# Both heads of a sorted pair in one transfer, and the decode steps of the seventh pair at other places

## The chip, the cores and the metric

The kernel runs on one core of a Trainium2 chip. The metric is the time of the program on the device in microseconds (us), lower is better. Beside it stand profiled executions, whose span runs from the first to the last instruction.

## The reference

Clustered attention, then a feed-forward block with hard-swish. Queries, keys and values are (batch 4, heads 8, 768 rows, 64 wide), with 16 centroids for each head.

```python
def _attn_ref(q, k, v, centroids):
    B, H, S, D = q.shape                       # 4, 8, 768, 64
    scale = 1.0 / np.sqrt(D)
    # q_n, k_n, c_n: rows divided by their norms
    q_assign = np.argmax(np.einsum('bhsd,hcd->bhsc', q_n, c_n), axis=-1)
    k_assign = np.argmax(np.einsum('bhsd,hcd->bhsc', k_n, c_n), axis=-1)
    mask = q_assign[:, :, :, None] == k_assign[:, :, None, :]
    scores = np.where(mask, scale * np.matmul(q, k.transpose(0, 1, 3, 2)), -1e9)
    attn = softmax(scores)                     # over the keys
    return np.matmul(attn, v)

def _moe_ref(x, w_in, w_out):                  # x: (3072, 512), from (B, S, H * D)
    h = x @ w_in                               # 512 -> 2048
    g = h * np.clip(h + 3.0, 0.0, 6.0) / 6.0
    return g @ w_out                           # 2048 -> 512
```

The weights w_in and w_out arrive as 64-bit floats and the kernel turns them into 32-bit floats itself.

## The kernel before

**Pairs.** The 32 heads are worked in 16 pairs. Two heads lie side by side on TensorE's 128 rows, and four pairs make the 512 inputs of one batch of the feed-forward block. Pairs 0 to 7 (the first two batches) take the full masked attention; pairs 8 to 15 are sorted by cluster first and then need only a band of the scores.

**The first stage, pairs 0 to 7.** A loop runs over n in steps of two, twelve values of n for each pair, so a pair has six double steps r = 0, 2, ... 10. A double step issues two blocks of scores (`ps`, L400, which takes one of two PSUM buffers), their exponentials on ScalarE (`ex`, L423), sums of the exponentials over the keys on GpSimd (`acc`, L430 and L433), and, two blocks later, the product with the values (`pv`, L443). Between them stand:
- the preparation of the next pair: transposes at r = 0 and 2 (`pqk`, L320), cluster scores at r = 4 (`pcs`, L337), the choice of the cluster at r = 6 (`route`: `pr` on TensorE, L348, then `mx` and `one_hot` on VectorE, L351 and L357), and the transposes of the one-hots at r = 8 and 10 (`po`, L379);
- the division, at r = 2 and 8: sums over partitions (`pd`, L467), a reciprocal and a product on VectorE (`rcp` L473, `num` L474). One double step later the result goes to memory, and ScalarE checks the reciprocals' range in place (L488, L489);
- the decode of the weights: 32 chunks of five steps each, `split` (L232 on VectorE, L228 on ScalarE, and the load of the chunk after next), `join` (L238), `power` (L248, and L244 on ScalarE), `rest` (L254), `total` (L259), and four weight sums after them. The table in `share` says how many steps a double step takes. They are issued at the end of the double step, behind its preparation;
- some up-projections of the first feed-forward block (`ph`, L607), at fixed n.

**The second stage, pairs 8 to 15.** Feed-forward items stand in a list, `fill`: for each block of tokens eight up-projections (`uX` and `uY`, L659) in a form that needs sums of weights (`tx`, loaded from `td` by ScalarE's queue, L548, two items ahead), and seven parts of the down-projection (`X` and `Y`, L698). One item is issued at each point of a plan, `late_plan`, and around it the steps of the sorted pairs, which `steps_of` places by hand: each pair starts 28 points after the last one. For a pair they are, in order: load the natural rows of q and k (`piece`), transpose them (`ps`, L919), cluster scores and choice, ranks (`order`, `positions`); load q, k and v again by rows (`qn`, `kvn`); scatter them to memory in sorted order (GpSimd, `scatter`, L1034); load the sorted rows (`piece`, `vs`), transpose, band attention, store the sorted result, gather it back (GpSimd, L1050), transpose and store for the feed-forward block.

**The order is written out by hand.** All is inside `tc.manual_schedule()`: each engine runs its instructions in the order of the program, and a transfer that waits in SP's queue holds up all behind it. Transfers from SP and from ScalarE take eight completion semaphores in turn, in the program's order.

**Loads of natural rows.** Each was one transfer for each head t of the pair, 192 KB. For the keys and values there were two steps, one for each head:

```python
for a, x in enumerate((k, v)):
    nc.sync.dma_start(st["kvn", g][:, :, t, a], natural(x, g, t))
```

Of the kernel before, what the change touches and what calls it, by code (L numbers as in the profile page):

```python
# [18 lines left out]
P = 128  # L19
# [100 lines left out]
def fast_path(ctx, tc, ok, q, k, v, centroids, moe_w_in, moe_w_out, out):  # L120
# [3 lines left out]
    nc = tc.nc  # L124
# [53 lines left out]
    st = {}  # L178
# [698 lines left out]
        for g in range(FIRST, NPAIR) for t in range(2) for name, w in (("qd", D), ("kvd", 2 * D), ("xsd", D))  # L877
    }

    def natural(x, g, t):  # L880
        b, h = divmod(2 * g, H)
        return x[b, h + t].rearrange("(p j) d -> p j d", p=P)

    def ranked(name, g, t, part=0):
        return rows[name, g, t].rearrange("(i p) d -> p i d", p=P)[:, :, part * D : (part + 1) * D]

    def load_piece(key, src):
        piece = st[key] = st["piecep"].tile([P, NCH, 2, D], F32, name="piece")
        for t in range(2):
            nc.sync.dma_start(piece[:, :, t], src(t))  # L890

    def load_natural(g, a):
        x = (q, k)[a]
        load_piece(("qk"[a] + "nat", g), lambda t: natural(x, g, t))

    def load_queries(g):
        qn = st["qn", g] = st["fromp"].tile([P, 2, NCH, D], F32, name="qn")
        for t in range(2):
            nc.sync.dma_start(qn[:, t], natural(q, g, t))

    def load_keys(g, t):
        if t == 0:
            st["kvn", g] = st["fromp"].tile([P, NCH, 2, 2, D], F32, name="kvn")
        for a, x in enumerate((k, v)):
            nc.sync.dma_start(st["kvn", g][:, :, t, a], natural(x, g, t))

    def load_ranked(g, a):
        if a < 2:
            load_piece(("qk"[a] + "s", g), lambda t: ranked(("qd", "kvd")[a], g, t))
            return  # L910
        vs = st["vs", g] = st["svp"].tile([P, 2, NCH, D], F32, name="vs")
        for t in range(2):
            nc.sync.dma_start(vs[:, t], ranked("kvd", g, t, 1))
# [278 lines left out]
    def steps_of(g):  # L1192

        first, last = g == FIRST, g == NPAIR - 1
        f = -3 if first else -5
        if first:
            plan = [
                (-38, load_queries), (-37, load_keys, 0), (-36, load_keys, 1), (-37, run_up),
                (-36, step_up), (-31, order), (-30, positions), (-20, lambda g: st.pop("signed")()),
            ]  # L1200
        else:
            plan = [
                (-46, load_natural, 0), (-45, load_natural, 1), (-38, turn_natural, 0), (-37, turn_natural, 1),
                (-36, cluster_scores), (-34, own_clusters), (-33, run_up), (-32, step_up), (-32, load_queries),
                (-31, load_keys, 0), (-29, order), (-29, positions), (-29, load_keys, 1),
            ]
        plan += [
            (-29 if first else -24, scatter, 0), (-29 if first else -24, scatter, 1), (-12, band_masks), (f, load_ranked, 0), (f, load_ranked, 1),
            (f + 1, load_ranked, 2), (-1, turn_ranked, 0), (0, turn_ranked, 1),
        ]  # L1210
        d = 1 if last else 2
        plan += [
            (d, band_scores, (0, 5), 1), (d + 2, band_scores, (2,), 3), (d + 4, band_scores, (4,)),
            (d + 4, band_values, 0), (d + 4, key_adds, 0, 1, 2), (d + 5, key_adds, 0, 3), (d + 7, band_values, 1),
            (d + 7, key_adds, 1, 1, 2), (d + 8, key_adds, 1, 3), (d + 10, band_sums),
            (12 if last else 14, band_divide), (14 if last else 16, keep_ranked),
            (15 if last else 23, gather), (28 if last else 37, turn_back),
        ]
        return [(g, *step) for step in plan]
# [28 lines left out]
    per_pair = 2 * NCH  # L1248
# [12 lines left out]
    READY, DECODED = per_batch + 2 * lag_d, 2 * per_batch  # L1261

    def share(n, r):


        if n < READY:
            return {0: 4, 2: 3, 4: 3, 6: 1, 8: 2, 10: 4}[r]
        if n < DECODED - per_pair:
            return {0: 6, 2: 5, 4: 4, 6: 3, 8: 5, 10: 5}[r]
        return {0: 6, 2: 5, 4: 4, 6: 1, 8: 3, 10: 4}[r]  # L1270

    HOLD = 6
# [13 lines left out]
    with tc.manual_schedule():  # L1286
# [19 lines left out]
        for n in range(0, total + lag_d + 2, 2):  # L1306
            g, r = divmod(n, per_pair)
# [25 lines left out]
            if n < total:  # L1333
                for step in decode[: share(n, r)]:
                    step()
                del decode[: share(n, r)]
# [389 lines left out]
```

## Time and profile before

| | us |
|---|---|
| median of three runs | 949.89 |
| lowest and highest | 947.76, 950.37 |
| profiled execution, its own time | 947.94 |
| its span, first to last instruction | 946.1 |
| TensorE busy | 928.3 |
| VectorE busy | 591.6 |
| GpSimd busy | 583.9 |
| ScalarE busy | 349.5 |

The granted TensorE clock was 0.998. In the profile PE is TensorE, PEld its weight loads, DVE VectorE, ACT ScalarE, POOL GpSimd, and SP the engine that only issues transfers; SPq and ACTq are the queues in which SP and ScalarE issue transfers and wait for semaphores. L12 is line 12 of the kernel before. A row of a timeline has start, duration, engine, line, operation, what it writes and reads, shapes and a count; in brackets at the end stands the idle time before it and what ended that. In a row of waits stand the total, how often, and the longest.

### The profile page before, as it was taken

What the parts mean: (1) busy time and instruction counts of PE and PEld (TensorE: products, weight loads), DVE (VectorE), ACT (ScalarE), POOL (GpSimd) and SP (SyncE); (2) the same over time, 40 slices, a digit from 0 to 9 for tenths busy, and PEclk for the clock granted to TensorE, in tenths of its full rate; (3) what the DMA queues carried; (4) which work ended last, traced back from release to release, by engine and by line L of the source; (5) the groups of instructions that cost most, each with busy time, mean ns of one, the idle gap of its engine ahead of it and who ended that gap; (6) DMA issues with size and microseconds to landing.
All of it is one profiled execution on the core that took longest, in us unless ns stands there. A gap on an engine that the chain in (4) does not pass through costs nothing.

```text
span 946.1 us, 17635 instructions
## 1 busy us (share of the span) xinstructions
PE 928.3 (98%) x6358; PEld 726.5 (77%) x6358; DVE 591.6 (63%) x1294; ACT 349.5 (37%) x731; POOL 583.9 (62%) x1314
## 2 busy tenths in 40 slices
PE   8999999989999999999999999999999999999997
PEld 5444444555798798797887988978888799999996
DVE  6789889899976375284483474564571554536261
ACT  5888877766112232233232132241331311212020
POOL 3878777769366677787777777777777060303030
PEclk9999999999999999999999999999999999999999
DMA  7345555361364648482683654754753233323120
GB/s 192 108 134 157 134 156 165 109 174 46 96 209 141 153 137 175 130 220 78 171 201 100 166 158 128 192 151 113 176 161 99 77 99 113 106 69 110 56 68 26
DMA packets 174351, 124.23 MB, mean 131 GB/s; under 512 B 134064, under 2 KB 152496, under 8 KB 174256
## 3 DMA queue, kind: packets, MB, share of 16 engines
q1 hardware_dynamic: 151936, 76.04, 31.2%
q10 hardware_dynamic: 13104, 34.38, 12.7%
q0 software_dynamic: 9216, 12.60, 4.4%
q8 instruction: 52, 0.85, 0.4%
q14 instruction: 43, 0.35, 0.1%
HBM read 94.67 MB, written 28.31 MB: 130 GB/s over the span
## 4 chain that ended last, share of the span: by engine, by line
PE 70%; DVE 2%; DMA 1%; ACT 0%; POOL 0%; issue 0%; SPq 0%; ACTq 0%
PE Y L698 18%; PE uY L659 15%; PE X L698 13%; PE uX L659 12%; PE pv L1116 3%; PE ps L1077 3%; PE ps L919 2%; PE pv L1077 1%; PE pd L1140 1%; PE pcs L337 1%; PE ps L1157 1%; DMA piece<-kvd 1%; DVE g_sb L649 0%; DVE g_sb L502 0%; DVE g_sb L670 0%; DVE sx L670 0%
## 5 line engine op out<-in xcount | busy, mean ns | idle before, releaser
L433 POOL TENSOR_TENSOR acc<-acc,ex 128x768 f32<-128x768 f32 x64 | 123.8, 1935 | 26.0 <-ACT ex L423 22.4
L1034 POOL DMA_INDIRECT qd<-qn,pos x96 | 96.3, 1003 | 44.9 <-issue 32.5
L1050 POOL DMA_INDIRECT xn<-xsd,pos x96 | 93.7, 976 | 48.8 <-DVE g_sb L649 27.1
L499 ACT ACTIVATE sx<-g_sb,half_c 128x512 f32<-128x512 f32 x88 | 63.7, 724 | 141.1 <-DVE g_sb L670 141.1
L649 POOL TENSOR_TENSOR g_sb<-g_sb 128x256 f32<-128x256 f32 x52 | 39.1, 773 | 123.6 <-DVE g_sb L502 122.6
L1034 POOL DMA_INDIRECT kvd<-kvn,pos x96 | 96.6, 1006 | 25.6 <-issue 25.6
L1026 POOL MEMSET w_low<- 128x1 f32 x864 | 90.9, 105 | 33.3
L705 DVE TENSOR_TENSOR y<-y,Y 128x256 f32<-128x256 f32 x48 | 20.2, 421 | 136.5 <-PE Y L698 135.7
L659 PE MATMUL uX<-xb,w_in_sb 128*128 128x128 f32 x704 | 93.0, 275 | 0.0
L698 PE MATMUL X<-w_out_sb,g_sb 128*128 128x256 f32 x384 | 90.6, 382 | 0.4 <-DVE g_sb L502 0.4
L698 PE MATMUL Y<-T,g_sb 128*128 128x256 f32 x384 | 88.0, 381 | 0.0
L698 PE MATMUL Y<-w_out_sb,g_sb 128*128 128x256 f32 x384 | 87.7, 380 | 0.0
L659 PEld LDWEIGHTS uX<-xb,w_in_sb 128*128 128x128 f32 x704 | 85.7, 192 | 0.0
L698 PEld LDWEIGHTS X<-w_out_sb,g_sb 128*128 128x128 f32 x384 | 70.9, 190 | 14.8 <-issue 3.9
L698 PEld LDWEIGHTS Y<-T,g_sb 128*128 128x128 f32 x384 | 72.1, 190 | 13.2 <-issue 3.9
L670 DVE TENSOR_TENSOR sx<-uX,sx 128x128 f32<-128x128 f32 x176 | 51.0, 290 | 49.3 <-ACT sx L677 45.7
L698 PEld LDWEIGHTS Y<-w_out_sb,g_sb 128*128 128x128 f32 x384 | 71.9, 190 | 10.6 <-issue 1.3
L400 PE MATMUL ps<-xf 64*128 64x384 f32 x384 | 78.6, 487 | 0.3 <-ACT ex L423 0.3
L423 ACT ACTIVATE ex<-ps 128x768 f32<-128x768 f32 x96 | 72.6, 802 | 4.6 <-PE ps L400 4.5
L443 PE MATMUL pv<-ex,vt 128*64 128x384 f32 x384 | 72.5, 499 | 0.0
L502 DVE SCALAR_TENSOR_TENSOR g_sb<-sx,g_sb 128x512 f32<-128x512 f32 x88 | 63.6, 725 | 3.4 <-ACT sx L499 3.4
L670 DVE TENSOR_TENSOR g_sb<-uY,sx 128x128 f32<-128x128 f32 (+1 forms) x176 | 65.5, 413 | 0.0
(196 smaller groups left out, 1805.5 us busy)
## 6 DMA issues: line engine op xcount, KB each, us to landing
tx<-td ACTq DMA_DIRECT2D x86, 384.0 KB, 3.5
raw<-in_moe_w_in_dram SPq DMA_DIRECT2D x16, 512.0 KB, 3.8
raw<-in_moe_w_out_dram SPq DMA_DIRECT2D x16, 512.0 KB, 3.2
xb<-xd SPq DMA_DIRECT2D x12, 512.0 KB, 4.3
out_dram<-y SPq DMA_DIRECT2D x44, 128.0 KB, 1.7
qk<-in_q_dram SPq DMA_DIRECT2D x18, 192.0 KB, 3.7
qk<-in_k_dram SPq DMA_DIRECT2D x18, 192.0 KB, 5.0
vt<-in_v_dram SPq DMA_DIRECT2D x16, 192.0 KB, 3.8
```

The lines of the kernel that those rows point to most:

```text
L400: nc.tensor.matmul(st["ps", n][:, t, 0:HALF], lhsT=x[r, NCH + j], rhs=x[r, hf * NHC : (hf + 1) * NHC], start=first, stop=last, skip_group_ ...
L423: nc.scalar.activation(out=ex, in_=sc, func=ACT.Exp, scale=SM_SCALE)
L433: nc.gpsimd.tensor_tensor(out=acc, in0=acc, in1=ex, op=ALU.add)
L443: nc.tensor.matmul(pv[t * D : (t + 1) * D], lhsT=vt[:, t, j], rhs=ex[:, t], start=(j == 0), stop=(j == NCH - 1),)
L499: nc.scalar.activation(out=r, in_=h, func=ACT.Relu, bias=half_c, scale=1.0 / 6.0)
L502: nc.vector.scalar_tensor_tensor(out=g, in0=r, scalar=1.0, in1=h, op0=ALU.min, op1=ALU.mult)
L659: nc.tensor.matmul(dst, lhsT=w[:, kt], rhs=x(kt), start=(kt == 0), stop=(kt == HK - 1))
L670: nc.vector.tensor_tensor(out=out_, in0=in0, in1=in1, op=ALU.add)
L698: nc.tensor.matmul(bank[:, half * HC : (half + 1) * HC], lhsT=g_sb[:, kind, i], rhs=w[:, i], start=(first and i == 0), stop=(last and i == ...
L1026: nc.gpsimd.memset(w_low, W_LOW)
L1034: i = nc.gpsimd.indirect_dma_start(out=rows[name, g, t], in_=src, in_offset=None, out_offset=bass.IndirectOffsetOnAxis(ap=pos[:, a, j, t : ...
L1050: nc.gpsimd.indirect_dma_start(out=xn[:, j, t], out_offset=None, in_=rows["xsd", g, t], in_offset=bass.IndirectOffsetOnAxis(ap=pos[:, 0, j ...
```

## The change

First, `natural` gives both heads of a pair at once, and the natural rows, queries, keys and values of a sorted pair are each loaded by one transfer of 384 KB instead of two of 192 KB. The two steps of `load_keys`, which loaded keys and values of head 0 and then of head 1, now load the keys of both heads and then the values of both; they stay at their points of the plan. The sorted rows (`ranked`) are still loaded head by head.

Second, the seventh pair (n from 72 to 83) gets a row of its own in the table of decode steps. The fifth pair's end and the sixth keep the old row.

```diff
-    def natural(x, g, t):
+    def natural(x, g, order="p j t d"):
         b, h = divmod(2 * g, H)
-        return x[b, h + t].rearrange("(p j) d -> p j d", p=P)
+        return x[b, h : h + 2].rearrange(f"t (p j) d -> {order}", p=P)
...
-    def load_piece(key, src):
+    def new_piece(key):
         piece = st[key] = st["piecep"].tile([P, NCH, 2, D], F32, name="piece")
-        for t in range(2):
-            nc.sync.dma_start(piece[:, :, t], src(t))
+        return piece
 
     def load_natural(g, a):
-        x = (q, k)[a]
-        load_piece(("qk"[a] + "nat", g), lambda t: natural(x, g, t))
+        nc.sync.dma_start(new_piece(("qk"[a] + "nat", g)), natural((q, k)[a], g))
 
     def load_queries(g):
         qn = st["qn", g] = st["fromp"].tile([P, 2, NCH, D], F32, name="qn")
-        for t in range(2):
-            nc.sync.dma_start(qn[:, t], natural(q, g, t))
-
-    def load_keys(g, t):
-        if t == 0:
+        nc.sync.dma_start(qn, natural(q, g, "p t j d"))
+
+    def load_keys(g, a):
+        if a == 0:
             st["kvn", g] = st["fromp"].tile([P, NCH, 2, 2, D], F32, name="kvn")
-        for a, x in enumerate((k, v)):
-            nc.sync.dma_start(st["kvn", g][:, :, t, a], natural(x, g, t))
+        nc.sync.dma_start(st["kvn", g][:, :, :, a], natural((k, v)[a], g))
...
+        if n < DECODED - 2 * per_pair:
+            return {0: 6, 2: 5, 4: 4, 6: 3, 8: 5, 10: 5}[r]
         if n < DECODED - per_pair:
-            return {0: 6, 2: 5, 4: 4, 6: 3, 8: 5, 10: 5}[r]
+            return {0: 8, 2: 3, 4: 3, 6: 2, 8: 4, 10: 8}[r]
         return {0: 6, 2: 5, 4: 4, 6: 1, 8: 3, 10: 4}[r]
```

More of the change, by code (lines that the diff above doesn't have):

```diff
@@ L878, in fast_path @@
     }
-    def natural(x, g, t):
+    def natural(x, g, order="p j t d"):
         b, h = divmod(2 * g, H)
-        return x[b, h + t].rearrange("(p j) d -> p j d", p=P)
+        return x[b, h : h + 2].rearrange(f"t (p j) d -> {order}", p=P)
     def ranked(name, g, t, part=0):
         return rows[name, g, t].rearrange("(i p) d -> p i d", p=P)[:, :, part * D : (part + 1) * D]
-    def load_piece(key, src):
+    def new_piece(key):
         piece = st[key] = st["piecep"].tile([P, NCH, 2, D], F32, name="piece")
-        for t in range(2):
-            nc.sync.dma_start(piece[:, :, t], src(t))
+        return piece
     def load_natural(g, a):
-        x = (q, k)[a]
-        load_piece(("qk"[a] + "nat", g), lambda t: natural(x, g, t))
+        nc.sync.dma_start(new_piece(("qk"[a] + "nat", g)), natural((q, k)[a], g))
     def load_queries(g):
         qn = st["qn", g] = st["fromp"].tile([P, 2, NCH, D], F32, name="qn")
-        for t in range(2):
-            nc.sync.dma_start(qn[:, t], natural(q, g, t))
-    def load_keys(g, t):
-        if t == 0:
+        nc.sync.dma_start(qn, natural(q, g, "p t j d"))
+    def load_keys(g, a):
+        if a == 0:
             st["kvn", g] = st["fromp"].tile([P, NCH, 2, 2, D], F32, name="kvn")
-        for a, x in enumerate((k, v)):
-            nc.sync.dma_start(st["kvn", g][:, :, t, a], natural(x, g, t))
+        nc.sync.dma_start(st["kvn", g][:, :, :, a], natural((k, v)[a], g))
     def load_ranked(g, a):
         if a < 2:
-            load_piece(("qk"[a] + "s", g), lambda t: ranked(("qd", "kvd")[a], g, t))
+            piece = new_piece(("qk"[a] + "s", g))
+            for t in range(2):
+                nc.sync.dma_start(piece[:, :, t], ranked(("qd", "kvd")[a], g, t))
             return
```

## The prediction

> **What bounds the kernel now.** I read the page first, then what TensorE waited for, then the timeline of each engine around the two longest of those waits, then the chain of waits.
>
> ```profile
> span 946.1 us, 17635 instructions
> ...
> PE 928.3 (98%) x6358; PEld 726.5 (77%) x6358; DVE 591.6 (63%) x1294; ACT 349.5 (37%) x731; POOL 583.9 (62%) x1314
> ...
> PE Y L698 18%; PE uY L659 15%; PE X L698 13%; PE uX L659 12%; PE pv L1116 3%; PE ps L1077 3%; PE ps L919 2%; PE pv L1077 1%; PE pd L1140 1%; PE pcs L337 1%; PE ps L1157 1%; DMA piece<-kvd 1%; DVE g_sb L649 0%; DVE g_sb L502 0%; DVE g_sb L670 0%; DVE sx L670 0%
> ```
>
> TensorE is busy for 928.3 of 946.1 us, and the diff takes no matmul away. So the change can move only the 17.8 us in which TensorE is idle. The profiled run took 947.94 us, 1.84 more than its span; the median of the three runs is 949.89, 1.95 above that run. I work out a difference and put it on the median.
>
> What TensorE waited for (total, times, longest) has two waits of 2 us, and both stand at things that the diff touches:
>
> ```profile
> PE po L379 <- DVE one_hot L357: 2.5, 2, 2.3
> PE uX L659 <- DMA tx<-td: 2.0, 1, 2.0
> ```
>
> The 2.3 us wait lies in the seventh pair: the turn of the routed one-hots (po) waits for VectorE. The 2.0 us wait lies among the sorted pairs: the weight sums tx come late, for a reason shown below.
>
> **Part one: the decode steps of the seventh pair.** Its six double steps (r = 0, 2, ... 10) held 6, 5, 4, 3, 5, 5 steps and now hold 8, 3, 3, 2, 4, 8: 28 both times, so nothing is added. Two steps go from r = 2 to r = 0, one from r = 4 to r = 6, two from r = 6 to r = 8, three from r = 8 to r = 10. The steps that load raw weights (every fifth) keep their places, so SP's queue is the same here. VectorE, whose queue the steps are moved in, now:
>
> ```profile
> 182.79 0.69 DVE L248 TENSOR_SCALAR wunit<-wtop 128x512 uint32<-128x512 uint32 x1
> 183.40 2.55 DVE L473 RECIPROCAL rcp<-pd 128x384 f32<-128x384 f32 x1
> 185.98 0.67 DVE L474 TENSOR_TENSOR num<-num,rcp 128x384 f32<-128x384 f32 x1
> 186.57 2.31 DVE L254 SCALAR_TENSOR_TENSOR wunit<-raw,wunit 128x512 f32<-128x512 uint32 x1
> ...
> 194.98 0.55 DVE L351 TENSOR_REDUCE mx<-pr 128x24 f32<-128x384 f32 x1
> 195.57 0.62 DVE L357 TENSOR_TENSOR one_hot<-pr,mx 128x192 bf16<-128x192 f32 x2
> ```
>
> The routing (mx, one_hot) starts only when VectorE has worked off the steps ahead of it, at 194.98. TensorE, ScalarE and GpSimd meanwhile:
>
> ```profile
> 189.64 0.55 PE L348 MATMUL pr<-ident,cs 128*128 128x128 f32 x3
> 190.12 0.34 PE L400 MATMUL ps<-xm 64*128 64x384 bf16 x2
> ...
> 193.18 0.81 PE L467 MATMUL pd<-acc,ones 128*64 128x384 f32 x4
> 196.25 0.51 PE L379 MATMUL po<-ident_q,one_hot 128*128 128x128 bf16 x6 [2.26 <-DVE one_hot L357]
> ```
>
> ```profile
> 187.66 0.51 ACT L488 ACTIVATE rcp<-rcp 128x384 f32<-128x384 f32 x1
> ...
> 188.90 1.49 ACT L423 ACTIVATE ex<-ps 128x768 f32<-128x768 f32 x2
> ```
>
> ```profile
> 182.51 8.05 POOL L433 TENSOR_TENSOR acc<-acc,ex 128x768 f32<-128x768 f32 x4
> 190.53 1.82 POOL L430 TENSOR_TENSOR acc<-ex 128x768 f32<-128x768 f32 x1
> ```
>
> L254, which reads two SBUF tiles, takes 2.31 while one of GpSimd's sums runs; L248, which reads one, takes 0.69, and I take that for an L254 that meets no sum. The four sums of the row take 2.01 each, so they end near 184.4, 186.5, 188.4 and 190.5.
>
> The new order, by these rows (a step of 0.69 is followed by the next after 0.6 to 0.7): L248 at 182.79; L254 at 183.5, held by the first sum to 184.4, ends 184.9; L259; the reciprocal at 185.5 instead of 183.40, because two decode steps now stand ahead of it; it ends at 188.1. L474 also reads two SBUF tiles and is held until the third sum ends: 188.85 instead of 186.65. Behind it wait two others. pr needs the PSUM buffer that the reciprocal frees: 188.1 is before 189.64, 1.5 us of room, free. ScalarE's in-place L488 waits for L474, and behind it in ScalarE's queue stand the exponentials: 187.66 becomes 188.95, so ex goes from 188.90 to 190.2 and its first half ends near 190.95. TensorE's ps, at 190.12 now, needs that half's buffer: it stalls 0.83 us, a wait that is new. VectorE goes on with L232, L238, L248 (188.9 to 191.05); its L254 then meets no sum, since L430 needs the delayed exponentials and starts after 191.6; L259 and L232 follow, and mx at 193.1, one_hot done at 194.3. TensorE finishes pd at 193.99 + 0.83 = 194.82 and finds one_hot ready. The stall goes from 2.26 to 0.83: **1.4 us gained**. From both sides: with L254 and L474 free of every sum, ex would be about 0.8 earlier and 2.2 us gained; with the second L254 held as long as in the row (2.31), one_hot would be done at 195.9 and 0.3 gained.
>
> [...]
>
> Later steps of the pair: the reciprocal of r = 8 comes two steps earlier, the three steps pushed to r = 10 stand behind a clip instead of ahead of it. VectorE has 196.1 to 212 to absorb them; nothing, unless it runs over, then 0.7 per step.
>
> **Part two: one transfer for both heads.** In the built program the transfers of SP and ScalarE take eight semaphores in turn, in program order: each waits until the eighth before it has landed. Five transfers go from each of seven pairs and three from the first sorted pair, 38 in all (403 to 365); bytes and piece sizes stay. The chain of waits, and SP's and ScalarE's queues, before the second wait:
>
> ```profile
> 476.28 4.90 DMA piece<-kvd
> 481.18 0.03 ACTq L548
> ```
>
> ```profile
> 475.70 1.43 SPq L890 DMA_DIRECT2D piece<-kvd  x2
> 477.19 2.15 SPq L913 DMA_DIRECT2D vs<-kvd  x2
> 479.50 1.26 SPq L899 DMA_DIRECT2D qn<-in_q_dram  x2
> 480.93 0.55 SPq L905 DMA_DIRECT2D kvn<-in_k_dram  x1
> 481.53 0.64 SPq L905 DMA_DIRECT2D kvn<-in_v_dram  x1
> ```
>
> ```profile
> 478.53 0.72 ACT L499 ACTIVATE sx<-g_sb,half_c 128x512 f32<-128x512 f32 x1 [2.57 <-DVE g_sb L670]
> 481.24 0.33 ACTq L548 DMA_DIRECT2D tx<-td  x1
> ```
>
> ```profile
> 486.04 0.68 PE L659 MATMUL uX<-xs,tx 128*128 128x128 f32 x4 [2.00 <-DMA tx<-td]
> ...
> 487.45 0.82 PE L919 MATMUL ps<-ident,piece 128*128 128x128 f32 x6
> ```
>
> ScalarE comes to this tx at 478.53 and issues it at 481.24, when a piece<-kvd lands that tx neither reads nor writes. That piece is the eighth before it: kvd, vs, the tx before this one, vs, qn, qn, k, v. Now qn is one transfer, k one for both heads, and the values come after the tx; the eighth before it is a tx, the last but one, that was issued ahead of the whole burst. So tx is issued 2.65 us earlier, at 478.6. It took at most 4.80 beside this burst (481.24 to 486.04); it lands by 483.4, and TensorE would want it at 484.04. **2.0 us gained**; if the burst held it to 6.1 us, 1.4.
>
> What is moved: the values of head 0 come one step later, with those of head 1, and the scatter of the tenth pair, whose queue (POOL's) goes on without rest, could wait for them:
>
> ```profile
> 311.14 0.65 SPq L905 DMA_DIRECT2D kvn<-in_v_dram  x1
> ```
>
> ```profile
> 314.79 0.95 POOL L1034 DMA_INDIRECT kvd<-kvn,pos  x1 [0.63 <-issue]
> ```
>
> The last value transfer was issued at 311.14, so the scatter has 3.6 us already; a landing like that tx's, 4.8, would cost GpSimd 1.2. Pieces like those issued from 475.70 on are turned at 487.45 (L919), 12 us behind their issue, so this hardly reaches the end. But TensorE, which gains, comes up to 3 us earlier against loads that GpSimd paces, and the later tx of the same bursts then wait a little for their eighth; I set **0.4 us** against the gain for that, between 0 and 1.3 (4.80 less the median 3.5 of a tx, in a row below).
>
> Sum: -1.4 - 2.0 + 0.4 = **-3.0 us**: 944.9 for the profiled run, **946.9** on the median, 0.32% less. About 0.3% (2.85 us) is what a measurement can tell from no change, so the forecast sits almost on that edge.
>
> **The rivals.** *tx was late by the crowd, not by the turn.* All 16 engines work through the burst; issued earlier, tx would just take longer. Then part one alone: -1.4, 948.5. For it: the 4.80 beside the burst. Against it: 2.65 us of waiting that the chain puts on another transfer.
>
> *The seventh pair only changes its wait.* If L488 comes later still, ps stalls for all that po gains: -2.0 + 0.4, 948.3. For it: 0.83 of new stall in my own working. Against it: it would take another 1.4 us on that path.
>
> *More goes than the profile shows.* The median run is 1.95 longer than the profiled one. If that, or most of it, is more waits of tx for their turn, which come and go between runs, 38 fewer transfers take 1.5 of it too: 945.4. For it: a wait of 2.65 that hangs on microseconds. Against it: nothing in one profile tells what other runs lose.
>
> *Slower: larger transfers crowd out tx.* In all a tx takes less than that one did:
>
> ```profile
> tx<-td ACTq DMA_DIRECT2D x86, 384.0 KB, 3.5
> ```
>
> So a burst costs it 1.3. If k and v of double size cost it 1.3 again each, that is 2.6 a burst, less the cover: from 478.53, when it can be issued, to 484.04, when it is wanted, are 5.5 us, 0.7 more than 4.80. About half of the eight pairs' bursts should meet up-projections (uX, uY: 27% of the chain, against 31% of the down product X, Y). So 4 x 1.9 = 7.6, less the 1.4 of part one: +6.2, 956.1. It decides from where each of four tx comes 1.8 later: 4 x 1.1 - 1.4 = +3.0.
>
> [...] No run here shows a transfer of both heads.
>
> **The chances.** Forecast 0.52, of it 0.38 beyond 0.3% and 0.14 within, as it sits on the edge; more goes 0.13, beyond; tx late by the crowd 0.12 and the seventh pair's new wait 0.08, both within; crowded out 0.15, of it 0.12 slower and 0.03 within. So faster 0.51, same 0.37, slower 0.12. The range: its low end has the more-goes case with the upper bound of part one (2.2 for 1.4) and nothing given back (945.4 - 0.8 - 0.4), and 0.4 for the spread of runs: 943.8; its high end lies 1.3 above no change, where the crowding has eaten both gains and one tx's delay more: 951.2.
>
> **What would show it.** Right: no wait of uX for tx near 484, tx issued when ScalarE is ready; po's wait gone, a wait of 0.8 of ps for ex at 190.9; 38 fewer issues, the same packets; TensorE busy 928. Wrong: po still waiting a microsecond or more, uX waits of 1 us in other bursts, or TensorE's idle time above 17.8.

## The result, and the profile after

The changed kernel takes **946.54 us** (median of six runs, 945.05 to 949.63); the kernel before, run beside it, 950.29 (six runs, 947.76 to 951.08). The ratio is 0.9963 with a 95% interval of 0.9948 to 0.9977, 3.5 us less. That is the predicted size, but the first profile does not show it where the prediction put it: the profiled execution was the longest of the six (949.63), while that of the kernel before lay at the short end of its own (947.94). The page of the changed kernel, and its waits of TensorE:

```profile
span 947.8 us, 17575 instructions
...
PE 929.6 (98%) x6358; PEld 728.1 (77%) x6358; DVE 589.8 (62%) x1294; ACT 349.5 (37%) x731; POOL 581.5 (61%) x1314
```

```profile
PE uX L659 <- DMA tx<-td: 2.2, 1, 2.2
PE ps L400 <- ACT ex L423: 2.1, 4, 0.8
PE uX L659 <- DVE sx L670: 1.9, 1, 1.9
```

The wait of `po` (2.3) is gone and a wait of `ps` for `ex` has come (0.8 the longest): part one, as forecast. But two waits of `uX` stand where there was one. TensorE's timeline at the three places, 190.97, 484.42 and 547.70 us:

```profile
190.97 0.34 PE L400 MATMUL ps<-xm 64*128 64x384 bf16 x2 [0.83 <-ACT ex L423]
...
194.03 0.81 PE L467 MATMUL pd<-acc,ones 128*64 128x384 f32 x4
194.78 0.51 PE L379 MATMUL po<-ident_q,one_hot 128*128 128x128 bf16 x6
...
484.42 0.68 PE L659 MATMUL uX<-xs,tx 128*128 128x128 f32 x4 [1.90 <-DVE sx L670]
484.94 1.67 PE L659 MATMUL uX<-xb,w_in_sb 128*128 128x128 f32 x8
...
547.70 0.68 PE L659 MATMUL uX<-xs,tx 128*128 128x128 f32 x4 [2.16 <-DMA tx<-td]
```

The wait at 484.42 is put down to VectorE, yet it is `tx` again: this `tx` landed at 484.28, 0.14 before the matmul, the same 0.14 that lies between the landing at 547.56 and 547.70. In the repetition on the first chip the same `uX` starts at 481.78, and the same instruction of VectorE only at 483.29, so the matmul does not need it. The releaser that the profile names can be a bystander that ended at the same moment.

ScalarE's timeline shows that `tx` no longer waits for its turn: it is issued 0.10 after ScalarE comes to it, where the kernel before waited 2.7 us. The windows show what followed the stall:

```profile
477.02 0.72 ACT L499 ACTIVATE sx<-g_sb,half_c 128x512 f32<-128x512 f32 x1 [2.57 <-DVE g_sb L670]
477.12 0.34 ACTq L548 DMA_DIRECT2D tx<-td  x1
```

```profile
484.00:485.20 1.20, 0.78 (x7) 0.81 (x8) 1.17 (x6) 0.00 (x0) 1.06 (x2) 1.00 1.07 276
485.20:488.60 3.40, 3.40 (x24) 3.28 (x23) 1.56 (x4) 1.67 (x3) 2.92 (x8) 0.50 0.65 188
488.60:495.00 6.40, 6.40 (x61) 6.13 (x60) 5.45 (x17) 1.73 (x4) 4.31 (x16) 1.00 0.32 86
```

(columns: window, its length, busy time of TensorE, weight load, VectorE, ScalarE, GpSimd, then TensorE's granted clock, the DMA share and GB/s; the DMA share adds up the packets' own times and can pass 1). So `tx` took 7.16 us to its landing, 477.12 to 484.28, and 7.30 to the matmul, where the kernel before had 4.66 and 4.80, and behind the stall the clock was halved for 3.4 us. Set side by side instruction by instruction, TensorE loses 1.28 us there against the kernel before. The two profiles differ by 1.69 us: -1.47 at `po`, -0.10 at the first `uX`, +1.28 by the clock, +2.16 at 547.70 and -0.37 from a wait of `ps` for `xsort` that is gone (0.4 in the waits of before) make +1.50. One execution of each is not the medians, and the experiments had to show what the typical run gains.

### The profile page after: what moved, and what is told of

It reads as the page before. It is cut to its first block, busy times and chain, and to the rows that moved or that the text cites. A ratio compares the mean times of both kernels' runs of the same rounds, so it can differ in the third digit from the quotient of the medians.

```text
span 947.8 us, 17575 instructions
## 1 busy us (share of the span) xinstructions
PE 929.6 (98%) x6358; PEld 728.1 (77%) x6358; DVE 589.8 (62%) x1294; ACT 349.5 (37%) x731; POOL 581.5 (61%) x1314
## 3 DMA queue, kind: packets, MB, share of 16 engines
q1 hardware_dynamic: 151328, 76.04, 31.2%
## 4 chain that ended last, share of the span: by engine, by line
PE 71%; DVE 2%; DMA 1%; POOL 0%; issue 0%; ACT 0%; ACTq 0%
PE Y L698 18%; PE uY L659 16%; PE X L698 13%; PE uX L659 12%; PE pv L1114 3%; PE ps L917 3%; PE ps L1075 3%; PE pv L1075 1%; DMA tx<-td 1%; PE pd L1138 1%; PE pcs L337 1%; PE ps L1155 1%; PE rk L999 0%; DVE g_sb L649 0%; DVE g_sb L670 0%; PE pdt L1151 0%
```

## The experiments

They ran on three chips in sets of four, each set with the kernel before beside it: 950.79 us on the first (25 runs), 954.79 on the second (35 runs, 948.8 to 960.4), 949.78 on the third (31 runs). Only kernels of one set are compared by their medians.

### First chip: each part alone, and both kernels again

The new share table in the kernel before:

```diff
+        if n < DECODED - 2 * per_pair:
+            return {0: 6, 2: 5, 4: 4, 6: 3, 8: 5, 10: 5}[r]
         if n < DECODED - per_pair:
-            return {0: 6, 2: 5, 4: 4, 6: 3, 8: 5, 10: 5}[r]
+            return {0: 8, 2: 3, 4: 3, 6: 2, 8: 4, 10: 8}[r]
```

> Part one alone: the kernel before with the new decode steps of the seventh pair, every transfer as it was. Prediction's theory: the wait of po for one_hot falls from 2.26 us to about 0, ps waits 0.83 us for ex, 1.4 us gained in this place, so 948.8 beside 950.3. The rival that the sorted pairs' stalls depend on small shifts of time: the place gains its 1.4 us all the same, but the whole may fall anywhere within 2 us of that.

The loads of the changed kernel with the old table:

```diff
-            return {0: 8, 2: 3, 4: 3, 6: 2, 8: 4, 10: 8}[r]
+            return {0: 6, 2: 5, 4: 4, 6: 3, 8: 5, 10: 5}[r]
```

> Part two alone: both heads in one transfer, decode steps as before. By the turn of the eight semaphores (prediction): tx is issued when ScalarE is ready and uX does not wait for it, 1.6 to 2.0 us gained, 948.5. By the crowd on the DMA engines: tx is issued earlier and lands no earlier, uX waits 2 us as before, no change, 950.3. In both the wait of po for one_hot stays at 2.26.

The changed kernel as it is:

> The changed kernel again, for a second profile of it. If the two waits of uX (1.90 and 2.16 us) and the 3.4 us at half clock of its first profile belong to every execution, they show again and the time is that of the first profile, 949.6. If they come and go, this profile has less than 2 us of such waits and the time is near the median, 946.5.

And the kernel before as it is:

> The kernel before again, unchanged, for a second profile of it and for the spread of the measurement. If the stalls of the sorted pairs come and go between executions, a profile of a typical execution (950.3 against 947.94 of the first profile) shows about 2.4 us more of waits for tx than the first one's 2.0. If not, the idle time of TensorE is again 17.8 us. Ratio 1.000 within 0.2%.

| kernel | median us | ratio to before, 95% interval |
|---|---|---|
| share table alone | 948.69 | 0.9982, 0.9973 to 0.9991 |
| loads alone | 948.48 | 0.9973, 0.9962 to 0.9983 |
| both (the changed kernel) | 945.91 | 0.9955, 0.9942 to 0.9968 |
| the kernel before again | 951.37 | 1.0006, 0.9994 to 1.0019 |

Both parts gain, and within these intervals they add up: 1.7 and 2.6 us by the ratios, 4.3 together and 4.3 measured. The waits of TensorE with the share table alone have part one as forecast, and the old wait for `tx`:

```profile
PE ps L400 <- ACT ex L423: 2.1, 4, 0.8
...
PE uX L659 <- DMA tx<-td: 2.0, 1, 2.0
```

The kernel before and the changed one, each profiled again, show that the waits for `tx` are not fixed: 3.1 here for before (2.0 in its first profile, so 1.1 more of the 2.4 more that were expected), and for the changed kernel 1.2 in all, with none near 484:

```profile
PE uX L659 <- DMA tx<-td: 3.1, 1, 3.1
PE po L379 <- DVE one_hot L357: 2.5, 2, 2.3
```

```profile
span 943.1 us, 17575 instructions
...
PE ps L400 <- ACT ex L423: 2.2, 4, 0.8
...
PE uX L659 <- DMA tx<-td: 1.2, 1, 1.2
```

With the loads alone the profile (950.31, its longest run) has the 2.26 of `po` with half a clock behind it, and waits of `uX` of 0.83, 1.47 and 1.23:

```profile
PE uX L659 <- DVE steps L950: 2.7, 2, 1.5
...
PE uX L659 <- DMA tx<-td: 0.8, 1, 0.8
```

The two that are put down to VectorE are waits for `tx` again, which landed 0.14 us ahead of either matmul (487.24 for 487.38, 548.00 for 548.14). So the first profile was no exception: a `tx` that is issued in time can still come late in the merged bursts. The expectation for this kernel had only two cases, no wait of `uX` or the old 2 us; the profile shows neither.

### Second chip: tx earlier, and the turn put back

`tx` three items ahead of its use instead of two, in the changed kernel and in the kernel before (the same edit):

```diff
-    txp = pool("txp", 3)
+    txp = pool("txp", 4)
...
-    expp = right(whole, "expp", 6)
+    expp = right(whole, "expp", 5)
...
-                    first_sums(u + 2)
+                    if u == HF:
+                        first_sums(u + 2)
+                    first_sums(u + 3)
...
-            ("rowp", 3), ("posp", 4),
+            ("rowp", 2), ("posp", 4),
```

> The changed kernel with tx issued three items ahead of its use instead of two (a fourth buffer for tx, one buffer less for the exponentials and one less for the rows of the sorted pairs, to make room). Theory (part two's gain is fewer and shorter waits of TensorE for tx, which come and go between executions, about 2.1 us of them in the median execution of the changed kernel): no wait of uX or uY for tx above 0.3 us anywhere, no half clock behind one, and a median of 944.3, 2.2 below the changed kernel. Rival (the waits for tx that the profiles show are made up elsewhere, or the median is longer for another reason): 946.5, like the changed kernel. If the buffers taken away cost something, a new wait at ps L400, pv L1116 or POOL would show it.

> The kernel before with the same: tx three items ahead, a fourth buffer for it, the same two buffers less. Theory (waits for tx make up about 4.4 us of the median of the kernel before): no wait for tx, the 2.26 us wait of po still there, median 946.1, and the distance to the changed kernel with the same edit shrinks from 4.2 to 1.8 us (1.4 of the seventh pair's steps and 0.4 of a wait of the turn of pieces for xsort). Rival (the merged transfers gain by something other than tx, such as less work on SP or GpSimd): the distance stays 4.2 us.

A tiny transfer behind each of the 38 transfers of both heads that stand for two (`take_turn()` follows L892, L896 and L901 of the changed kernel):

```diff
+    spare = dram.tile([40, 1], F32, name="spare")
+    taken = []
+
+    def take_turn():
+        nc.sync.dma_start(spare[len(taken) : len(taken) + 1], q[0, 0, 0:1, 0:1])
+        taken.append(1)
```

> The changed kernel with a transfer of four bytes, DRAM to DRAM, behind every merged one, so that 403 transfers take the eight semaphores in turn again, as before, while the bytes stay merged. Theory of the turn (tx gains because it no longer waits for a transfer of the burst): tx waits for its eighth-before again or for a tiny one that stands in the queue behind the burst; part two's gain is lost, 948.7, like the new share table alone. Rival by bytes in one transfer (the gain is that of the larger transfers): 946.5, like the changed kernel.

And the natural pieces in two transfers again:

```diff
-        nc.sync.dma_start(new_piece(("qk"[a] + "nat", g)), natural((q, k)[a], g))
+        piece, src = new_piece(("qk"[a] + "nat", g)), natural((q, k)[a], g)
+        for t in range(2):
+            nc.sync.dma_start(piece[:, :, t], src[:, :, t])
```

> The changed kernel with the natural pieces of queries and keys (L892) in two transfers each as before; only the rows for the scatter (qn, kvn) are merged, so 22 of the 38 transfers stay away. Theory of the turn: the tx that waited for its turn in the kernel before stood among qn and kvn, so nearly all of part two stays: 946.6 to 947.1. Rival (the natural pieces' double transfers made the rest of the tx wait): 947.7 or more, half of part two gone.

| kernel | median us | ratio to before, 95% interval |
|---|---|---|
| changed, tx three ahead | 952.08 | 0.9987, 0.9962 to 1.0012 |
| before, tx three ahead | 955.57 | 1.0005, 0.9979 to 1.0031 |
| changed, tiny transfers added | 960.22 | 1.0068, 1.0040 to 1.0096 |
| changed, natural pieces in two | 955.08 | 0.9992, 0.9958 to 1.0027 |

The medians cannot be held against the expectations, since this chip is 4 us slower for the kernel before, and its intervals are as wide as the effects. In the four profiles TensorE loses time in the bursts of the second stage, part of it in steps of about 0.3 us in which it waits for no engine and no load ("issue"); the cause of that is open. The natural pieces in two leave four waits of `uX` for `tx`, 5.3 us in all, and decide nothing between the two theories on them. The kernel with the tiny transfers takes 5.4 us more than the kernel before, where the theory of the turn gives 1.6 less (948.7 for 950.3). Its profile has no wait of ScalarE for a turn; SyncE's queue shows instead that each stands between the large ones and holds them back:

```profile
484.74 1.65 SPq L904 DMA_DIRECT2D qn<-in_q_dram  x1
486.43 0.61 SPq L884 DMA_DIRECT2D spare<-in_q_dram  x1
487.21 0.65 SPq L910 DMA_DIRECT2D kvn<-in_k_dram  x1
487.90 1.07 SPq L884 DMA_DIRECT2D spare<-in_q_dram  x1
489.02 0.66 SPq L910 DMA_DIRECT2D kvn<-in_v_dram  x1
```

The values leave 1.8 us behind the keys instead of 0.65 (476.79 and 477.44 in the changed kernel). So that kernel tests the price of an issue as much as the turn, and says nothing clean of the latter. What does stand is that the changed kernel with an early `tx` has no wait for `tx` at all in its profile. The time that this gives was measured on the third chip.

### Third chip: the early tx again, and what its buffers cost

> The changed kernel once more, on the chip of the kernels beside it, since on the second chip the kernel before took 954.8 us instead of 950.5 and TensorE lost some us of idle time at every burst of loads. Theory (what the change gains does not hang on the chip): 3.7 to 4.7 us less than the kernel before. Rival (larger transfers lose what they gain where the bursts go slower): less than 2.7 us.

> The changed kernel with tx three items ahead again. Theory (its waits for tx are some 2 us of a median execution and nothing takes their place): 1.5 to 2.5 us below the changed kernel beside it, no wait for tx in its profile. Rival (the buffers taken away, or another wait, eat that up): within 1 us of the changed kernel.

> The kernel before with tx three items ahead again. Theory (its waits for tx are some 4 us): 3 to 4 us below the kernel before, and 1.8 above the changed kernel with the same edit. Rival (the waits for tx are made up elsewhere): within 1 us of the kernel before.

The fourth is the changed kernel with only the smaller pools:

```diff
-    expp = right(whole, "expp", 6)
+    expp = right(whole, "expp", 5)
...
-            ("rowp", 3), ("posp", 4),
+            ("rowp", 2), ("posp", 4),
```

> The changed kernel with only the two buffers less (one of the exponentials, one of the sorted rows) that the kernels with tx three items ahead go without; tx two items ahead as in the changed kernel. It prices the buffers: if they are spare, within 0.5 us of the changed kernel beside it; if they cost what the earlier tx brings, 1.5 us or more above it.

| kernel | median us | ratio to before, 95% interval |
|---|---|---|
| changed | 948.14 | 0.9982, 0.9969 to 0.9996 |
| changed, tx three ahead | 945.58 | 0.9955, 0.9938 to 0.9971 |
| before, tx three ahead | 951.75 | 1.0016, 1.0000 to 1.0032 |
| changed, smaller pools alone | 947.37 | 0.9974, 0.9955 to 0.9992 |

The changed kernel alone gains 1.7 us here by the ratio, not the 3.7 to 4.7 that were expected; its rival, less than 2.7, has the size, but no run shows that slower bursts are the cause.

An early `tx` takes 2.6 us off the changed kernel (1.8 off the one with the smaller pools), as the theory had it, and nothing off the kernel before, against the theory: there the kernel is 2.0 slower than before (1.5 by the ratio, 0 to 3.0). The two kernels with an early `tx` lie 6.2 us apart, and 3.5 on the second chip, not the 1.8 that were expected, so the merged loads gain by something else than the waits for `tx`. ScalarE's timeline of the kernel before with an early `tx` shows by what:

```profile
478.80 0.72 ACT L499 ACTIVATE sx<-g_sb,half_c 128x512 f32<-128x512 f32 x1 [2.57 <-DVE g_sb L672]
481.74 0.33 ACTq L548 DMA_DIRECT2D tx<-td  x1
482.16 0.27 ACT L679 COPY sx<-uX 128x128 f32<-128x128 f32 x1 [2.64 <-DMA piece<-kvd]
```

in its chain of waits:

```profile
476.34 5.32 DMA piece<-kvd
481.66 0.02 issue
481.68 0.02 ACTq L548
...
482.16 0.28 ACT sx L679
...
483.20 0.22 DVE runs L954
...
487.51 0.20 DVE steps L954
```

and in TensorE's timeline:

```profile
485.48 0.82 PE L921 MATMUL ps<-ident,piece 128*128 128x128 f32 x6
488.25 0.26 PE L990 MATMUL rk<-every,upto 128*128 128x1 bf16 x4 [1.95 <-DVE steps L954]
```

`tx` is not wanted for another item, but its issue still waits 2.7 us for its turn (the landing of the eighth transfer before it), until `piece<-kvd` lands. ScalarE works in program order, so the copy `sx` behind it waits too, then VectorE's `runs` and `steps`, then `rk` on TensorE: 1.95 us, with half a clock behind it (the `uY` at 489.29 takes 1.10 us, the same four matmuls 0.61 at 482.35). Set side by side instruction by instruction with the first profile of the kernel before, this one gains 2.2 us where that one waited for `tx` (486.04) and loses 3.7 by the end of the half clock: 1.5 us slower in this stretch. That is one execution of each, and it fits the medians. What the smaller pools cost the kernel before was not measured. In the changed kernel with the same early `tx` ScalarE passes without a stop:

```profile
479.32 0.72 ACT L499 ACTIVATE sx<-g_sb,half_c 128x512 f32<-128x512 f32 x1 [2.57 <-DVE sx L672]
479.40 0.33 ACTq L548 DMA_DIRECT2D tx<-td  x1
479.95 0.26 ACT L679 COPY sx<-uX 128x128 f32<-128x128 f32 x1
```

So there are two delays, one behind the other. The turn holds ScalarE (2.7 us); the merged transfers take that away here. Beside the crowd, the other transfers of the burst, the bytes of `tx` come late (7.16 us from issue to landing in the first profile of the changed kernel); an earlier issue covers that. Taken away alone, each leaves the other to be waited for; together they give 945.58, **the fastest of all versions on that chip**, 0.9955 of before. The wait of ScalarE for `piece<-kvd`, 2.3 to 2.6 us, stands in the profiles of four kernels with unmerged loads (before, its repetition, the share table alone, before with an early `tx`), and near that place in none with merged loads. The fifth profile with unmerged loads, the early `tx` on the second chip, does not have it either, so it comes and goes as well. Four kernels with merged loads have one wait of ScalarE of 8 us for a transfer elsewhere; no wait of TensorE of 0.3 us stands beside it. The smaller pools cost the changed kernel nothing that can be measured.

## Why the prediction was right or wrong

**TensorE as the bound: right.** Its busy time was 928.3 and is 927.4 to 930.2 in the three profiles of the changed kernel, high in the two that have a half clock behind a stall.

**Part one: right in each step.** VectorE's timeline of the changed kernel:

```profile
183.47 1.36 DVE L254 SCALAR_TENSOR_TENSOR wunit<-raw,wunit 128x512 f32<-128x512 uint32 x1
...
185.47 2.55 DVE L473 RECIPROCAL rcp<-pd 128x384 f32<-128x384 f32 x1
188.06 0.78 DVE L474 TENSOR_TENSOR num<-num,rcp 128x384 f32<-128x384 f32 x1
...
190.93 0.69 DVE L254 SCALAR_TENSOR_TENSOR wunit<-raw,wunit 128x512 f32<-128x512 uint32 x1
...
192.98 0.55 DVE L351 TENSOR_REDUCE mx<-pr 128x24 f32<-128x384 f32 x1
193.56 0.62 DVE L357 TENSOR_TENSOR one_hot<-pr,mx 128x192 bf16<-128x192 f32 x2
```

The reciprocal stands at 185.47 (185.5 forecast), `mx` at 192.98 (193.1), `po` at 194.78 (194.82), the new stall is 0.83. The two L254 take 1.36 beside a sum of GpSimd and 0.69 with none, so the 0.69 that the prediction took for an L254 beside no sum is what this trace shows, and its lower bound of 0.3, with 2.31 for the second, is out. The trace gains 1.47 at `po` for the 1.4 forecast; the table alone gained 0.9 to 2.6 by its interval. It is also worth more than its wait where half a clock follows the 2.26 us stall, as in the profile of the loads alone (0.50 for 3.40 us).

**Part two: the turn right, the landing wrong.** `tx` is issued when ScalarE comes to it, as worked out. The step that failed is the next, that `tx` lands by 4.80, at most 6.1, after its issue: it took 7.16, and the wait of 2.0 became 1.90 in that execution. The late `tx` of the loads alone and of the repetition took 5.7 to 6.7. So at this place the rival "late by the crowd" came true. The 0.4 given back in other bursts, with 1.3 as its end, was mis-sized as well: 2.16 at 547.70, 1.2 in the repetition. What I had not counted is the other side of the turn: the same 2.7 us hold every copy of ScalarE behind the issue, and the early `tx` in the kernel before shows that this alone costs TensorE 1.95. The loads alone gained 2.6 us (1.6 to 3.6) for the 1.6 forecast. The sum of 3.0 met the measured 3.5 with wrong terms in its second half, so that it came so near is in part luck. Two of the signs of being wrong did appear in the first profile, a wait of `uX` of over 1 us in another burst (2.16) and an idle time of TensorE of 18.2 us, above 17.8; in the repetition the one long wait is 1.2 and the idle time 15.7.

**Beside the merged loads `tx` starts late.** The DMA view of the changed kernel from the issue of `tx` (477.1) for 2.4 us has only the queues of SyncE (q1) and GpSimd (q0); that of ScalarE (q10) moves nothing:

```profile
q1 hardware_dynamic: 1496, 0.66, 103.1%
q0 software_dynamic: 38, 0.03, 5.4%
```

In a quiet stretch, 909.22 to 911.00, `tx` has 53 packets through 1.8 us after its issue. By the trace's packets its first one moves 1.0 us after the issue there, 1.9 in the burst of the kernel before (issue at 481.24) and 2.5 here; from that packet to the landing it takes 2.8 us before and 4.6 here. So beside the merged loads `tx` both starts later and moves more slowly. What holds its start these views do not tell.

Part of the 4.6 is a straggler. The landing of `tx` is the last of sixteen steps of its semaphore; fifteen had come by 483.21, the last came 1.07 us later. At 547.70 the last is 1.05 late as well (546.51 and 547.56), and 1.07 at the 487.38 of the loads alone; in the kernel before it is 0.03 (485.87 and 485.90). Without it the stall of 1.90 would have been about 0.8. What held that one step is open.

**The rivals.** Slower by crowding did not decide, though late `tx` are there (7.16 us to the landing at 484.28, where the kernel before had 4.66): it needed four `tx` 1.8 us late, and a profile of the changed kernel has at most two long waits for `tx`. "More goes than the profile shows" fits the first chip (4.3 us) and "late by the crowd" the third (1.7); the second had no run of the changed kernel alone. The intervals of the result and of the third chip overlap (0.9948 to 0.9977, 0.9969 to 0.9996), but how much the gain hangs on the chip stays open. So does how often a typical run of either kernel meets each wait, since a run without a profile shows none.

**A small miss.** The packets are not the same: 608 fewer on SyncE's queue (151936 before, 151328 after), 16 for each of the 38 transfers.

## What to carry to other kernels

A transfer that is issued from an engine's own queue can wait for a semaphore that has nothing to do with its data, and then everything behind it on that engine waits as well (here the issue of `tx` 2.7 us for `piece<-kvd`, and behind it the copy `sx` 2.64); look at the engine's next instruction, not only at who wants the data. When two delays stand one behind the other, removing one may show little until the other goes (on the third chip the early `tx` took 2.6 us off the changed kernel and nothing off the kernel before): try each alone and both together. And where waits come and go, a profile of each side is an anecdote: compare medians of many runs, and use profiles for the mechanism.

## What the runs showed of the hardware

In the first profile of the changed kernel a stall of TensorE of 1.90 us was followed by 3.4 us at half clock (0.50 from 485.20 to 488.60). That cost another 1.3 us there, and such a stretch cost 1.6 to 1.7 in three others set side by side in the same way (the loads alone, the changed kernel on the third chip, the kernel before with an early `tx` there). In the fourteen profiles, leaving out the first 50 us, eight of 17 stalls of 1.8 us or more were followed so, and none of 13 between 1.0 and 1.8. Stalls of one length went both ways: the 2.26 us at `po` were followed so in the profile of the loads alone and not in the first profile of the kernel before, where the clock was 1.00 from 190 to 940. The longest, the 3.1 us of the kernel before in its repetition, was not followed so either (its mean clock was 0.999; 3.4 us at half clock alone would make it 0.998). What decides is open. The windows of the kernel with the loads alone, from 1.4 us behind its 2.26 us stall at 195.46:

```profile
196.87:200.27 3.40, 3.40 (x14) 1.13 (x12) 3.31 (x3) 3.34 (x10) 0.29 (x1) 0.50 1.23 256
200.27:204.00 3.73, 3.73 (x19) 2.93 (x16) 3.66 (x4) 0.27 (x1) 3.65 (x3) 1.00 0.35 138
```
